# Attention and gated MLP: the opening of the kernel in finer steps

## The chip, the core and the metric

One core of a Trainium2 chip runs the whole program. The metric is the device time of one execution in microseconds (us); smaller is better. Engines are named as in the profile: PE is TensorE (PEld its weight loads), DVE is VectorE, ACT is ScalarE, POOL is GpSimd, SP is SyncE, which here only issues DMAs, in a fixed order, each at its turn.

## What is computed

Causal attention over 4 batches of 12 heads (448 positions, head size 64, fp32), followed by a gated MLP on the 1792 tokens of 768 features. The scales of `q` and `k` don't change the work.

```python
scores = scale * np.matmul(q, k.transpose(0, 1, 3, 2))
scores = np.where(mask, -1000000000.0, scores)          # causal
attn = np.exp(scores - max); attn = attn / (sum(attn) + 1e-09)
out = np.matmul(attn, v)
x = out.transpose(0, 2, 1, 3).reshape(4 * 448, 768)
gate = 1.0 / (1.0 + np.exp(-(x @ w_gate)))
result = (gate * (x @ w_val)) @ w_out
```

## The kernel before

**Units of work.** Attention goes by pairs of heads, 24 pairs, 6 to a batch. The MLP goes by batches: batches 0 and 1 each as a unit of its own (lines 582 to 653), 2 and 3 together (from line 720). Each product of the MLP is three matmuls, because x and the weights are split into a high and a low part (line 594).

**A pair, in the opening.** The six pairs of batch 0 are the opening; nothing of the MLP can run before their features are there. For a pair, `load` (L274, L279) fetches the queries and keys into `raw` and an extra piece into `sm`, `load_v` (L285) the values into `vr`. `products` (L387) computes four blocks of scores, i = 0 to 3, for 128 queries each (64 for the last) against 128, 256, 384 and 448 keys, for both heads z. Blocks 0 and 1 share one PSUM tile per head and are one step of PE; blocks 2 and 3 are steps of their own. `softmax` then has, per block and head, one masking and maximum on DVE (L410), one exponential on ACT (L417), and per pair two reciprocals of the sums on DVE (L426, L428) and a scaling on POOL (L438). `trans` (L313) transposes the scaled blocks in four groups g of four 128x128 squares into a PSUM tile `t`, of which there are two, and `empty` (L319 to L324) copies each group from PSUM to `pt` in SBUF, on ACT for the groups in the tuple `EV` (line 39) and on DVE for the others. `pv` (L337, L342) multiplies by the values, and `features` copies the result out as `xh` (ACT, L355) and the remainder `xl` (DVE, L356).

**Later pairs** (from pair 6) compute all four blocks in one step (`wscore`), and `shift` transposes on DVE (L453) and through DRAM: one write to `pd` (L461), four reads into `pt` (L464). `wpv` (L481) multiplies by the values.

**Weights.** `weight` (from line 548) fetches a 64-bit weight tile (L559), puts its two words together (ACT L563, DVE L565 and L567), stores the fp32 tile to `wdram` for the second unit (L570), and splits it (ACT L575, then POOL or DVE L577).

**The order.** Every operation is put into `Plan` with a cost, the buffers that it reads and writes with keys inside them, and a due time. `Plan.order` (line 156) pulls due times back from successors, adds the entries of `NUDGE` by the number of the operation, and then picks on each engine the ready operation that is due first. The instructions are issued to each engine in the order found; the waits come from the buffers. Since operations are numbered as they are put in, a table `NUDGE` holds for one list of operations alone.

```python
cols = (0, 4 * WQ, 2 * S) if n == 0 else (0, 2 * S)      # line 271: the first pair's load in two pieces
EV = (1, 3)                                              # line 39: groups of transposes that ACT copies
```

Of the kernel before, what the change touches and what calls it, by code (L numbers as in the profile page):

```python
# [15 lines left out]
B, H, S, D = 4, 12, 448, 64  # L16
# [21 lines left out]
WC = 512  # L38
EV = (1, 3)
BUFS = dict(w64=3, wd=2, wr=3, ws=3, sm=4, raw=3, pt=2, gt=5, vr=2, st=4, tb=1)  # L40
# [7 lines left out]
NUDGE = {  # L48
# [7 lines left out]
}  # L56
# [151 lines left out]
def kernel(  # L208
# [59 lines left out]
    def load(n):  # L268
        j = pairs[n]
        j["raw"] = r = new("raw", [128, 2 * S], F32, BUFS["raw"])  # L270
        cols = (0, 4 * WQ, 2 * S) if n == 0 else (0, 2 * S)
        for e, (a, c) in enumerate(zip(cols, cols[1:])):
            keys_ = (e,) if n == 0 else (0, 1)
            plan.op("SP", dma(128 * (c - a) * 4), lambda a=a, c=c: nc.sync.dma_start(  # L274
                out=r.t[:, a:c], in_=qkt[n][:, a:c]), writes=[(r, *keys_)], extra=2.8)
# [12 lines left out]
    def score(n, blocks, due):  # L288
# [8 lines left out]
        j["sp"].update({i: (sp, woff(i) - woff(blocks[0])) for i in blocks})  # L297
        needs = [(j["raw"], *((0,) if blocks[-1] == 1 else (0, 1)))] + ([(j["sm"][1], "x")] if blocks[-1] == 3 else [])
        burst((qk_cost(blocks), lambda: products(j, blocks), needs, [(p,) for p in sp]), due)
        return lambda: softmax(j, blocks)  # L300
# [69 lines left out]
    def products(j, blocks):  # L370
        r, x = j["raw"], j["sm"][1]
        first = r is pairs[0]["raw"]
        q0 = lambda i: WQ * i + (S if first and i > 1 else 0)
        k0 = 2 * WQ if first else S
        for i in blocks:
# [13 lines left out]
    def wscore(n, due):  # L389
# [4 lines left out]
        j["sp"] = {0: (a, 384), 1: (b, 0), 2: (a, 0), 3: (b, 256)}  # L394
        burst((1.95, lambda: products(j, range(NB)), [(j["raw"], 0, 1), (j["sm"][1], "x")], [(p,) for p in a + b]), due)
        return lambda: softmax(j, range(NB))

    def softmax(j, blocks):
        mn, su, r_ = j["mn"], j["sum"], j["r"]
        for i in blocks:  # L400
# [4 lines left out]
            for z in range(2):  # L405
# [6 lines left out]
                    op0=ALU.add, op1=ALU.min, accum_out=mn.t[:, to, i:i + 1],  # L412
                ), [(sp[z],), (mask, "end") if last and z else (mask,)] + ([(mn, (1, i))] if last and z else []),
                    [(sm, (i, z) if last else i), (mn, (to, i))])
            for z in heads:
                sm = j["sm"][z]
                plan.op("ACT", act(ne, 0, 1) + 0.01, lambda z=z, sm=sm, i=i, ne=ne, off=off: nc.scalar.activation(  # L417
                    out=sm.t[:, off:off + ne], in_=sm.t[:, off:off + ne], func=ACTF.Exp, scale=-1.0,
                    bias=mn.t[:, z, i:i + 1], accum_out=su.t[:, z, i:i + 1],
                ), [(mn, (z, i))], [*([(sm, (i, 0), (i, 1))] if last else []), (sm, i), (su, (z, i))], extra=0.1)  # L420
# [625 lines left out]
def _lay(q, k, v, moe_w_gate, moe_w_val, moe_w_out):  # L1046
# [5 lines left out]
    x = qkt[0].copy()  # L1052
    qkt[0] = np.concatenate([x[:, :2 * WQ], x[:, S:], x[:, 2 * WQ:S]], axis=1)
    qkt = np.concatenate([qkt, ex], axis=2)
# [40 lines left out]
```

## Time and profile before

| what | before |
| --- | --- |
| median of 3 runs | 622.55 us (621.22 to 623.70) |
| the profiled execution's own time | 620.8 us |
| its span in the profile | 619.1 us |
| granted clock of PE | 1.00 in every stretch |
| busy share of PE, PEld, DVE, ACT, POOL | 98%, 86%, 71%, 54%, 50% |

The profiled execution took 1.7 us more than its span, which is what lies around the first and the last instruction. A busy share is an average over the opening, the middle and the end of the program, which have different limits; the stretches have to be read one by one. Times in rows are us from the start of the span.

### The profile page before, as it was taken

What the parts mean: (1) busy time and instruction counts of PE and PEld (TensorE: products, weight loads), DVE (VectorE), ACT (ScalarE), POOL (GpSimd) and SP (SyncE); (2) the same over time, 40 slices, a digit from 0 to 9 for tenths busy, and PEclk for the clock granted to TensorE, in tenths of its full rate; (3) what the DMA queues carried; (4) which work ended last, traced back from release to release, by engine and by line L of the source; (5) the groups of instructions that cost most, each with busy time, mean ns of one, the idle gap of its engine ahead of it and who ended that gap; (6) DMA issues with size and microseconds to landing.
All of it is one profiled execution on the core that took longest, in us unless ns stands there. A gap on an engine that the chain in (4) does not pass through costs nothing.

```text
span 619.1 us, 11867 instructions
## 1 busy us (share of the span) xinstructions
PE 606.9 (98%) x4182; PEld 531.5 (86%) x4182; DVE 439.7 (71%) x1048; ACT 335.6 (54%) x754; POOL 310.6 (50%) x350
## 2 busy tenths in 40 slices
PE   6999999999999999999999999999999999999997
PEld 3578888898888888888888899989999989999996
DVE  5897999889855546544648766577754688999752
ACT  6996765675634755555558644434333443657420
POOL 5650534614300676767676676658664666611200
PEclk9999999999999999999999999999999999999999
DMA  8688999998999999878786886855533213534321
GB/s 299 203 308 314 344 370 378 376 397 320 364 396 339 321 365 344 293 245 319 269 323 247 281 311 238 276 199 189 179 110 95 77 52 103 159 117 142 112 75 60
DMA packets 54348, 153.35 MB, mean 248 GB/s; under 512 B 6032, under 2 KB 12432, under 8 KB 51984
## 3 DMA queue, kind: packets, MB, share of 16 engines
q1 hardware_dynamic: 54288, 152.59, 69.6%
q8 instruction: 33, 0.54, 0.3%
q14 instruction: 27, 0.22, 0.1%
HBM read 109.31 MB, written 43.25 MB: 246 GB/s over the span
## 4 chain that ended last, share of the span: by engine, by line
PE 89%; DMA 4%; DVE 3%; ACT 2%; issue 1%; POOL 0%; SPq 0%; DVEq 0%; ACTq 0%; POOLq 0%
PE m L594 39%; PE m L807 19%; PE s L807 10%; PE t L807 7%; PE m L481 5%; PE s L387 4%; PE t L387 2%; DMA raw<-in_qkt_dram 2%; DMA pd<-tb 1%; DMA vr<-in_vt_dram 1%; PE t L313 1%; ACT sm L417 1%; DVE wr L567 1%; DVE sm L410 1%; POOL sm L438 0%
## 5 line engine op out<-in xcount | busy, mean ns | idle before, releaser
L761 POOL TENSOR_TENSOR wl<-room,wh 128x384 fp32r<-128x384 f32 x84 | 98.0, 1190 | 56.0 <-ACT wh L760 56.0
L438 POOL TENSOR_SCALAR sm<-sm,r 128x384 f32<-128x384 f32 (+3 forms) x165 | 94.1, 591 | 63.6 <-DVE r L428 50.2
L594 PE MATMUL m<-xh,wh 128*128 128x448 f32 x288 | 107.3, 372 | 0.0
L594 PE MATMUL m<-xh,wl 128*128 128x448 f32 x288 | 105.3, 366 | 0.0
L594 PE MATMUL m<-xl,wh 128*128 128x448 f32 x288 | 105.2, 365 | 0.0
L417 ACT ACTIVATE sm<-sm,mn 128x384 f32<-128x384 f32 (+3 forms) x168 | 87.6, 524 | 18.6 <-DVE mn L410 15.2
L577 POOL TENSOR_TENSOR wl<-wr,wh 128x768 fp32r<-128x768 f32 x38 | 70.6, 1872 | 24.1 <-ACT wh L575 20.8
L575 ACT CAST wh<-wr 128x768 fp32r<-128x768 f32 x72 | 59.8, 832 | 33.4 <-DVE wr L567 15.0
L760 ACT CAST wh<-room 128x384 fp32r<-128x384 f32 x84 | 39.8, 511 | 52.5 <-PE s L807 12.7
L410 DVE CUSTOM_DVE_ANT_0 sm<-s,mask 128x128 f32<-128x128 f32 (+3 forms) x108 | 42.5, 408 | 25.8 <-PE s L387 25.7
L594 PEld LDWEIGHTS m<-xh,wh 128*128 128x128 f32 x288 | 54.1, 188 | 6.6 <-issue 1.6
L594 PEld LDWEIGHTS m<-xh,wl 128*128 128x128 f32 x288 | 54.1, 188 | 4.5
L594 PEld LDWEIGHTS m<-xl,wh 128*128 128x128 f32 x288 | 54.1, 188 | 4.1
L594 PE MATMUL m<-gh,wh 128*128 128x448 f32 x144 | 53.3, 370 | 0.0
L594 PE MATMUL m<-gh,wl 128*128 128x448 f32 x144 | 52.6, 365 | 0.0
L594 PE MATMUL m<-gl,wh 128*128 128x448 f32 x144 | 52.6, 365 | 0.0
L624 POOL TENSOR_TENSOR gl<-gt,gh 128x448 fp32r<-128x448 f32 x24 | 28.9, 1208 | 37.4 <-ACT gh L623 27.3
L807 PE MATMUL m<-pt,wh 128*128 128x448 f32 x150 | 44.8, 367 | 0.2 <-DVE xl L676 0.2
L453 DVE STREAM_TRANSPOSE room<-sm 128x384 f32<-128x384 f32 (+2 forms) x84 | 35.4, 449 | 8.8 <-POOL sm L438 8.4
L387 PE MATMUL s<-raw 64*64 64x128 f32 (+3 forms) x432 | 35.7, 390 | 4.6 <-DMA raw<-in_qkt_dram 3.5
L481 PEld LDWEIGHTS m<-pt,vr 128*64 128x64 f32 x720 | 33.5, 137 | 7.8 <-issue 4.3
L577 DVE TENSOR_TENSOR wl<-wr,wh 128x768 fp32r<-128x768 f32 x34 | 33.5, 984 | 7.9 <-ACT wh L575 7.4
(177 smaller groups left out, 1373.7 us busy)
## 6 DMA issues: line engine op xcount, KB each, us to landing
room<-in_wp_dram SPq DMA_DIRECT2D x36, 768.0 KB, 7.4
pt<-pd SPq DMA_DIRECT2D x72, 256.0 KB, 5.6
wr<-wdram SPq DMA_DIRECT2D x45, 384.0 KB, 4.6
room<-wdram SPq DMA_DIRECT2D x45, 384.0 KB, 3.6
wdram<-wr SPq DMA_DIRECT2D x36, 384.0 KB, 7.6
pd<-room SPq DMA_DIRECT2D x12, 1024.0 KB, 4.7
raw<-in_qkt_dram SPq DMA_DIRECT2D x23, 448.0 KB, 5.9
vr<-in_vt_dram SPq DMA_DIRECT2D x24, 256.0 KB, 5.3
```

What stands on the lines that cost most here:

```text
L387: nc.tensor.matmul(out=sp[z].t[c:c + 64, o:o + ne], lhsT=q, rhs=k)
L410: plan.op("DVE", dve(n), lambda z=z, i=i, sp=sp, sm=sm, n=n, o=o, f=f, lo=lo, to=to, first=first: nc.vector.tensor_tensor_reduce(out=sm.t[ ...
L417: plan.op("ACT", act(ne, 0, 1) + 0.01, lambda z=z, sm=sm, i=i, ne=ne, off=off: nc.scalar.activation(out=sm.t[:, off:off + ne], in_=sm.t[:, ...
L438: plan.op("PL", 0.24 + w / 1200, lambda sm=sm, e=e, o=o, w=w, z=z: nc.gpsimd.tensor_scalar(out=sm.t[:, o:o + w], in0=sm.t[:, o:o + w], sca ...
L453: plan.op("DVE", dve(128 * c) + 0.03, lambda sm=sm, i=i, o=o, c=c, at=at: nc.vector.transpose(out=tv()[:, :, at:at + 32 * c].rearrange("p ...
L481: nc.tensor.matmul(out=vp.t[64 * z:64 * z + 64, i * WQ:i * WQ + rows(i)], lhsT=v.t[:, c, z], rhs=src, start=(c == 0), stop=(c == i))
L575: plan.op("ACT", act(768), lambda: nc.scalar.copy(hi_.t, t.t), [(t,)], [(hi_,)])
L577: plan.op(eng, cost, lambda: at.tensor_tensor(out=lo_.t, in0=t.t, in1=hi_.t.bitcast(F32), op=ALU.subtract), [(t,), (hi_,)], [(lo_,)], lock ...
L594: nc.tensor.matmul(out=ps.t[:, :S], lhsT=a.t[:, k, :], rhs=b.t if isinstance(b, Buf) else b(), start=(first and z == 0), stop=(last and z ...
L760: plan.op("ACT", act(w), lambda: nc.scalar.copy(f(hi_.t), x()), [(src, at)], [(hi_, e)])
L761: plan.op("PL", 0.97, lambda: nc.gpsimd.tensor_tensor(out=f(lo_.t), in0=x(), in1=f(hi_.t).bitcast(F32), op=ALU.subtract), [(src, at), (hi_ ...
L807: nc.tensor.matmul(out=ps.t[:, :S], lhsT=a.t[:, kw, :], rhs=b.at, start=bool(first and z == 0), stop=bool(last and z == 2), skip_group_che ...
```

## The change

The first pair's `qkt` is laid out on the host as 128 queries, all 448 keys, and the other 320 queries, and fetched in three DMAs: 256 columns (128 queries and 128 keys), 448 columns, 192 columns. Block 0 of the first pair is a step of PE of its own, due 0.3 us before block 1, and the scores' tile is tracked by blocks. `EV` is (1,): of the four groups of a pair in the opening ACT copies one and DVE three. The planner's cost of an exponential rises by 0.08 us. `NUDGE` is another table, since the operations are numbered anew.

```diff
-EV = (1, 3)
+EV = (1,)
...
-        cols = (0, 4 * WQ, 2 * S) if n == 0 else (0, 2 * S)
+        cols = (0, 2 * WQ, S + 2 * WQ, 2 * S) if n == 0 else (0, 2 * S)
...
-            keys_ = (e,) if n == 0 else (0, 1)
+            keys_ = (e,) if n == 0 else (0, 1, 2)
...
-        needs = [(j["raw"], *((0,) if blocks[-1] == 1 else (0, 1)))] + ([(j["sm"][1], "x")] if blocks[-1] == 3 else [])
-        burst((qk_cost(blocks), lambda: products(j, blocks), needs, [(p,) for p in sp]), due)
+        needs = lambda i: [(j["raw"], *range(min(i + 1, 3)))] + ([(j["sm"][1], "x")] if i == 3 else [])
+        if n < 1 and len(blocks) > 1:
+            for i in blocks[:-1]:
+                plan.op("PE", qk_cost((i,)), lambda i=i: products(j, (i,)), needs(i), [(p, i) for p in sp], due - 0.3)
+        here = blocks[-1:] if n < 1 else blocks
+        burst((qk_cost(here), lambda: products(j, here), needs(here[-1]), [(p, *here) for p in sp]), due)
...
-                ), [(sp[z],), (mask, "end") if last and z else (mask,)] + ([(mn, (1, i))] if last and z else []),
+                ), [(sp[z], i), (mask, "end") if last and z else (mask,)] + ([(mn, (1, i))] if last and z else []),
...
-                plan.op("ACT", act(ne, 0, 1) + 0.01, lambda z=z, sm=sm, i=i, ne=ne, off=off: nc.scalar.activation(
+                plan.op("ACT", act(ne, 0, 1) + 0.09, lambda z=z, sm=sm, i=i, ne=ne, off=off: nc.scalar.activation(
...
-    qkt[0] = np.concatenate([x[:, :2 * WQ], x[:, S:], x[:, 2 * WQ:S]], axis=1)
+    qkt[0] = np.concatenate([x[:, :WQ], x[:, S:], x[:, WQ:S]], axis=1)
```

**What moves.** Lines of the change stand up to 3 lower or 1 higher than before (L387 is L390, L410 is L413, L274 is L273, L285 is L284). First place: PE at the start of the program, the scores of the first pair (`s` and `m` are PSUM tiles of scores, one per head, the number tells buffers apart; the brackets name the semaphores waited on). Before:

```order
L387 MATMUL s_315<-raw_289 64x128 [waits DMAHW0_49]
L387 MATMUL s_316<-raw_289 64x128
L387 MATMUL s_315<-raw_289 64x128
L387 MATMUL s_316<-raw_289 64x128
L387 MATMUL s_315<-raw_289 64x256
L387 MATMUL s_316<-raw_289 64x256
```

And of the change:

```order
L390 MATMUL s_316<-raw_289 64x128 [waits DMAHW0_49]
L390 MATMUL s_317<-raw_289 64x128
L390 MATMUL s_316<-raw_289 64x128
L390 MATMUL s_317<-raw_289 64x128
L390 MATMUL s_316<-raw_289 64x256 [waits DMAHW1_49,DVE_49]
L390 MATMUL s_317<-raw_289 64x256 [waits DVE_49]
```

The order is the same, but block 1 (256 keys) now waits for the second DMA and, since it writes to the tile that DVE reads block 0 from, for DVE.

Second place: SP's queue at the start, where every load stands. Before:

```order
L274 DMA raw<-in_qkt_dram 128x512
L274 DMA raw<-in_qkt_dram 128x384
L279 DMA sm<-in_qkt_dram 128x288
L274 DMA raw<-in_qkt_dram 128x896
L279 DMA sm<-in_qkt_dram 128x288
L285 DMA vr<-in_vt_dram 128x512
```

And of the change:

```order
L273 DMA raw<-in_qkt_dram 128x256
L273 DMA raw<-in_qkt_dram 128x448
L273 DMA raw<-in_qkt_dram 128x192
L278 DMA sm<-in_qkt_dram 128x288 x2
L284 DMA vr<-in_vt_dram 128x512 x2
L273 DMA raw<-in_qkt_dram 128x896 x3
```

The load of pair 1 (896 columns) was the fourth DMA and is the eighth, behind both extra pieces and both values.

Third place: SP's queue in the middle of unit 0, at the values of a later pair (the pair whose `pt` is read). Before:

```order
L461 DMA pd<-tb 128x2048
L559 DMA room<-in_wp_dram 128x1536 x2
L464 DMA pt<-pd 128x512 x4
L285 DMA vr<-in_vt_dram 128x512
L570 DMA wdram_2322<-wr 128x768
```

And of the change:

```order
L464 DMA pd<-tb 128x2048
L562 DMA room<-in_wp_dram 128x1536
L284 DMA vr<-in_vt_dram 128x512
L573 DMA wdram_2252<-wr 128x768
L562 DMA room<-in_wp_dram 128x1536
L467 DMA pt<-pd 128x512 x4
```

The values `vr` went ahead of the second weight and of the four reads of `pt`; at the pair after this one they did so too.

## Rows read from the trace of the kernel before

**Rows 1.** Busy time by stretch: stretch, length, engines with instructions, clock, DMA share, GB/s

```profile
core 0: us, PE busy (x) PEld busy (x) DVE busy (x) ACT busy (x) POOL busy (x), PEclk, DMA share, GB/s
0.00:15.00 15.00, 9.58 (x100) 5.74 (x100) 8.58 (x46) 10.27 (x32) 7.59 (x24) 1.00 0.86 300
...
5.20:47.62 42.42, 39.41 (x410) 25.99 (x404) 38.38 (x148) 38.70 (x112) 24.77 (x41) 1.00 0.83 284
...
54.20:180.00 125.80, 124.01 (x876) 109.81 (x874) 110.26 (x263) 81.60 (x169) 46.11 (x59) 1.00 0.97 362
180.00:360.00 180.00, 180.00 (x1487) 156.31 (x1487) 108.73 (x383) 103.52 (x264) 114.63 (x140) 1.00 0.87 309
```

**Rows 2.** Timeline, 0 to 30 us: start, length, engine, line, operation, [idle before <-releaser]

```profile
0.80 0.86 SPq L274 DMA_DIRECT2D raw<-in_qkt_dram  x2
...
2.18 0.43 SPq L274 DMA_DIRECT2D raw<-in_qkt_dram  x1
...
3.47 1.56 PE L387 MATMUL s<-raw 64*64 64x128 f32 x16 [3.47 <-DMA raw<-in_qkt_dram]
...
5.20 0.29 DVE L410 CUSTOM_DVE_ANT_0 sm<-s,mask 128x128 f32<-128x128 f32 x1 [5.20 <-PE s L387]
...
5.62 0.42 DVE L410 CUSTOM_DVE_ANT_0 sm<-s,mask 128x256 f32<-128x256 f32 x1
...
6.36 0.56 DVE L410 CUSTOM_DVE_ANT_0 sm<-m,mask 128x384 f32<-128x384 f32 x1
...
8.93 0.25 DVE L410 CUSTOM_DVE_ANT_0 sm<-s,mask 128x128 f32<-128x128 f32 x1
```

**Rows 3.** DMA issues of the first pairs: KB each, us from issue to landing

```profile
raw<-in_qkt_dram SPq DMA_DIRECT2D x1, 256.0 KB, 2.6
...
raw<-in_qkt_dram SPq DMA_DIRECT2D x1, 192.0 KB, 2.6
...
raw<-in_qkt_dram SPq DMA_DIRECT2D x1, 448.0 KB, 5.1
```

**Rows 4.** Timeline, one copy on DVE and one on ACT, each with its follower

```profile
32.37 0.69 DVE L324 COPY pt<-t 128x512 f32<-128x512 f32 x1
...
32.62 0.57 ACT L322 COPY pt<-t 128x512 f32<-128x512 f32 x1
...
33.02 0.39 DVE L410 CUSTOM_DVE_ANT_0 sm<-s,mask 128x224 f32<-128x224 f32 x1
33.09 0.62 ACT L417 ACTIVATE sm<-sm,mn 128x384 f32<-128x384 f32 x1
```

**Rows 5.** Timeline, the end of the opening: last copies, and the last two products with values

```profile
46.93 0.69 DVE L324 COPY pt<-t 128x512 f32<-128x512 f32 x1
...
47.26 1.52 PE L337 MATMUL s<-pt,vr 128*64 128x384 f32 x12
47.37 0.59 ACT L322 COPY pt<-t 128x512 f32<-128x512 f32 x1 [0.48 <-PE t L313]
...
49.07 1.47 PE L337 MATMUL s<-pt,vr 128*64 128x384 f32 x12
```

**Rows 6.** Timeline of PE, the two longest waits behind the opening

```profile
162.59 2.00 PE L481 MATMUL m<-pt,vr 128*64 128x128 f32 x40 [1.23 <-DMA vr<-in_vt_dram]
...
179.94 2.00 PE L481 MATMUL m<-pt,vr 128*64 128x128 f32 x40 [0.56 <-DMA vr<-in_vt_dram]
```

**Rows 7.** SP's queue in the timeline (values' issues), and the chain (last `pt` issue)

```profile
155.64 0.47 SPq L285 DMA_DIRECT2D vr<-in_vt_dram  x1
...
171.99 1.38 SPq L464
...
173.41 0.44 SPq L285 DMA_DIRECT2D vr<-in_vt_dram  x1
```

**Rows 8.** DMA issues at 155.2, 155.6, 172 and 173.4 us: KB each, us to landing

```profile
pt<-pd SPq DMA_DIRECT2D x1, 256.0 KB, 6.8
...
vr<-in_vt_dram SPq DMA_DIRECT2D x1, 256.0 KB, 6.9
...
pt<-pd SPq DMA_DIRECT2D x1, 256.0 KB, 7.2
...
vr<-in_vt_dram SPq DMA_DIRECT2D x1, 256.0 KB, 6.4
```

More of the change, by code (lines that the diff above doesn't have):

```diff
@@ L372, in products @@
         first = r is pairs[0]["raw"]
-        q0 = lambda i: WQ * i + (S if first and i > 1 else 0)
-        k0 = 2 * WQ if first else S
+        q0 = lambda i: WQ * i + (S if first and i else 0)
+        k0 = WQ if first else S
         for i in blocks:
@@ L394, in wscore @@
         j["sp"] = {0: (a, 384), 1: (b, 0), 2: (a, 0), 3: (b, 256)}
-        burst((1.95, lambda: products(j, range(NB)), [(j["raw"], 0, 1), (j["sm"][1], "x")], [(p,) for p in a + b]), due)
+        burst((1.95, lambda: products(j, range(NB)), [(j["raw"], 0, 1, 2), (j["sm"][1], "x")], [(p, 0, 2) for p in a] + [(p, 1, 3) for p in b]), due)
         return lambda: softmax(j, range(NB))
```

13 rows, old and new, of the table NUDGE are left out of this document.

## Prediction

> **What bounds the kernel now.** I read the busy time by stretch first, then the waits of PE, then the timeline of the opening, then the DMAs at the two places where PE waits. The stretches show three stages [rows 1]. From 180 us on PE is busy for the whole of 180.00 us out of 180.00: nothing to win there, only to lose. From 54 to 180 us PE is idle for 125.80 - 124.01 = 1.8 us, and the DMA engines are busy for 0.97 of the time at 362 GB/s: this stage is close to the limit of the DMAs, and 1.23 + 0.56 = 1.8 us of PE's idle time stands before two products that wait for the values of their pair [rows 6]. The opening, from DVE's first softmax operation at 5.20 us to the end of DVE's last copy at 47.62, is 42.42 us long; in it PE is idle for 3.0 us, DVE for 4.0 and ACT for 3.7 [rows 1]. So three engines there are over 90% busy and wait for each other in turn; none has room for much more, and PE could win 3.0 us at the very most. The granted clock is 1.00 throughout, the upper of its two levels (2.4 GHz), so the clock explains nothing here.
>
> Two lengths cannot be moved much, therefore: the opening, and the two waits of 1.8 us. All that the change can win is 3.0 + 1.8 us and what the first load saves, about 5 us or 0.8%.
>
> **First load.** Before, 256 KB land 2.6 us after their issue and 192 KB also 2.6 us [rows 3]. The first piece is now 128 KB. From the two equal rows the gain is 0; from the rate of the first stretch, 300 GB/s [rows 1], 128 KB less are 0.44 us. I take 0.2, between the two. [...]
>
> **Block 0 alone.** PE starts at 3.47 and DVE's first operation at 5.20 [rows 2]. The order of waits shows why: DVE had to wait for seven matmuls, four of block 0 and three of block 1. These took 1.73 us. Four of seven by count would be 0.99 us, by columns (512 of 1280) 0.69; I take 0.8 and DVE starts at 3.47 - 0.2 + 0.8 = 4.1, which is 1.1 us sooner. But PE now waits for DVE: block 1 writes to the tile that DVE still reads. DVE needs 0.21 us per head (two rows of block 0 between 5.20 and 5.62) [rows 2], so block 1 starts at about 4.3, needs the other 0.9 us, and DVE goes on at 5.2 to 5.3 instead of 5.62. Block 2 now comes behind that on PE. Its three matmuls of 384 columns have 1152 columns against 1280 in 1.73 us, so 1.0 to 1.5 us, and DVE gets to block 2 at 6.3 to 6.8; before it was 6.36 [rows 2]. So what is won at the first operation is spent at the third: by then DVE has waited about 1.1 us that it did not wait before. Net for the first pair 0, between -0.3 and +0.4.
>
> **Pair 1's load goes back in the queue.** It was issued at 2.18 and landed at 2.18 + 5.1 = 7.3 us [rows 2, 3], with 592 KB issued ahead of it. Now 1248 KB are ahead. At 300 GB/s [rows 1] the 656 KB more cost 2.2 us, so it lands at up to 9.5; if the DMAs issued behind it shared the time before as well, the least is about 8.5. DVE began pair 1 at 8.93, when the scores were long there [rows 2]. PE needs about 0.9 us for the two blocks, so DVE begins pair 1 at 9.5 to 10.4 instead. I take a wait of 0.9 us for DVE and ACT.
>
> **Six copies from ACT to DVE.** A copy ends its turn on DVE after 33.02 - 32.37 = 0.65 us and on ACT after 33.09 - 32.62 = 0.47 us [rows 4]. Six pairs, one copy each: DVE gets 3.9 us more, ACT 2.8 us less. ACT's relief only helps if ACT was what the others waited for. Here a rule speaks against the change. The Trainium skill (Perfetto Trace Analysis, Optimizing Scalar/DVE Operations) gives DVE a larger overhead per access to PSUM than ScalarE (about 125 against 51 ns) and advises to offload from DVE to Scalar when DVE is saturated; the rows agree with its order, and by it this edit would be a loss, which is the second rival below.
>
> **The sum for the opening.** DVE's work from its first operation to its last copy was 38.4 us [rows 1]; it is now 38.4 + 3.9 = 42.3. The weights' operations on DVE and ACT inside the opening only move to later places in it; their number up to the last copy is the same. From 4.1 us on, without any idle time, the last copy would end at 46.4. I add the 1.1 us of the first pair, the 0.9 us of the second and 0.4 us for the other four, because a queue that always has a copy ready hardly runs dry (in the last 12 us of the opening DVE already works like this). That is 48.8. Before, the last copy, on ACT, ended at 47.37 + 0.59 = 47.96, and the last product with values began at 49.07, held up by the one before it on PE [rows 5]. It now begins at 48.8: the opening wins **0.3 us**. With the 4.0 us of idle time that DVE has now [rows 1] added to the two new waits it would end at 46.4 + 1.1 + 0.9 + 3.7 = 52.1 and lose 3.0; with PE's idle time all gone it would win 3.0 + 0.2. Those are the ends.
>
> **The values ahead of `pt`.** Two products waited for `vr`, which was issued behind the four reads of `pt` [rows 6, 7]. The first `vr` went out at 155.64 and landed 6.9 us later, at 162.5; the last `pt` went out at about 155.2 and landed 6.8 us later, at 162.0 [rows 7, 8]. Without the wait for `vr` the next to be late is `pt`, so 0.5 of the 1.23 us goes. At the second place `vr` landed at 173.41 + 6.4 = 179.8 and the last `pt` at 171.99 + 7.2 = 179.2 [rows 7, 8]; all of the 0.56 us goes. Sum **1.1 us**, at most 1.8 if `pt` also comes sooner, and 0 if in the full DMA stage another transfer becomes late in their place. In the change the values also stand ahead of a weight that held up the queue.
>
> All else in the new due times I cost at nothing: behind 180 us PE has work at hand always, and a place more or less in its order costs nothing as long as the weights come in time; if they don't, the price is a new wait like those two, 0.5 to 1.2 us each.
>
> Together -0.3 - 1.1 = -1.4 us against the profiled execution's 620.8, so 619.4. The median of the three runs is 622.55, 1.75 us above that execution; on its scale the forecast is **621.1 us**.
>
> **The rivals.** (All on the median's scale.)
>
> - *PE bound in the opening* (0.27). DVE takes the copies without holding anyone up, ACT's 2.8 us are what the others had waited for, and PE loses its 3.0 us of idle time. For it: PE's work in the opening is 39.4 of 42.4 us, and DVE's order now mixes copies with softmax more finely. Against it: DVE's sum above. Time: -3.0 - 0.2 - 1.1 to -1.8, about 618.0.
> - *DVE too full* (0.20). Every copy that PE waits for (there are two `t` tiles, so the third group of a pair waits for the copy of the first) stands behind softmax on one engine. It decides from the point at which DVE's last copy ends later than 49.1 us. With today's idle time kept the last copy ends at 52.1 and the time is +3.0, 625.6; with the gain at `vr` 624.5, with pair 1's load later still 626.5.
> - *Given back* (0.15). The opening ends sooner, but the stage to 180 us runs at the pace of the DMAs (0.97 busy) and PE waits at the same places until the same data are there. Then the time is that of before, 622.5. Against it: the weights' loads are tied to the opening's progress and come sooner with it.
>
> **How the numbers follow.** My forecast has 0.38, with a range of its own from 619.9 to 622.3. 0.5% is 3.1 us, about what a measurement of this kernel can tell from no change. Faster by more than that needs 619.4 or less: the first rival, 0.27. Slower by more needs 625.7: of the second rival somewhat over half, 0.13. The rest, 0.60, is within 0.5%. The range for 8 times in 10 takes in most of the first rival and the nearer part of the second: 617.4 to 625.0.
>
> **What would show it.** In the profile after: DVE's first operation near 4.1 us and a wait of DVE for PE right behind it; pair 1's load landing at 8.5 to 9.5 and DVE's first operation of pair 1 behind 9.5; DVE's idle time in the opening down to 2.4 us from 4.0; the last copy at about 48.8 and the last product with values right behind; no wait for `vr` near 160 and 179 us, and a short one for `pt` in its place. I am wrong on DVE if its idle time stays near 4 us or the last copy ends before 47; wrong on the full DMA stage if PE's idle time from the end of the opening to 180 us is again 1.8 us or more; and wrong on all that I cost at nothing if PE is no longer busy all the time behind 180 us.

## The result: 0.56% slower, and the profile after

Over 8 executions each, the median went from 621.95 to 625.33 us; the ratio is 1.0056, with a 95% interval of 1.0034 to 1.0078. That is 3.4 us more, where 1.4 us less had been forecast. The profiled execution of the change took 625.79 us with a span of 624.1 (before 619.1). In the tables "6th product" is the start on PE of the sixth pair's product with values, which ends the opening (before 49.07 [rows 5]).

Busy time by stretch in the change (stretch, length, engines with instructions, granted clock, DMA share, GB/s); the last two lines, from a narrower query, show the clock behind PE's longest wait:

```profile
0.00:15.00 15.00, 9.11 (x76) 5.31 (x76) 6.97 (x35) 7.82 (x24) 5.80 (x19) 0.89 0.81 268
15.00:55.00 40.00, 38.61 (x437) 26.49 (x436) 37.37 (x122) 31.14 (x86) 22.36 (x34) 1.00 0.76 250
54.20:180.00 125.80, 124.64 (x886) 109.50 (x879) 110.53 (x263) 79.67 (x167) 41.97 (x59) 1.00 0.96 362
340.00:390.00 50.00, 47.73 (x347) 42.66 (x346) 39.34 (x89) 26.50 (x63) 29.37 (x28) 1.00 0.74 265
...
10.00:11.00 1.00, 1.00 (x20) 0.66 (x23) 0.25 (x2) 0.00 (x0) 1.00 (x3) 0.85 1.02 292
11.00:12.00 1.00, 1.00 (x9) 0.10 (x2) 0.79 (x6) 0.87 (x4) 1.00 (x3) 0.50 0.90 304
```

Three places differ from [rows 1]. From 0 to 15 us the granted clock is 0.89 instead of 1.00, and in 11 to 12 us it is 0.50, the lower level (1.2 GHz). From 54.2 to 180 us PE's idle time fell from 1.8 to 1.16 us. And from 340 to 390 us PE, which before was busy there without a gap (first row below), is idle for 2.27 us (50.00 - 47.73). Three rows of the kernel before, to set beside those of the change:

```profile
340.00:390.00 50.00, 50.00 (x360) 45.08 (x359) 35.36 (x73) 26.42 (x59) 33.62 (x30) 1.00 0.76 269
...
7.31 0.88 PE L387 MATMUL m<-raw 64*64 64x384 f32 x8 [0.46 <-DMA raw<-in_qkt_dram]
...
330.89 0.68 DVE L686 TENSOR_TENSOR tb<-xl,tb 128x448 fp32r<-128x448 f32 x1 [0.24 <-ACT tb L681]
```

The timeline of the change, PE's and DVE's rows of the opening and the new waits:

```profile
2.99 0.71 PE L390 MATMUL s<-raw 64*64 64x128 f32 x8 [2.99 <-DMA raw<-in_qkt_dram]
4.22 1.33 PE L390 MATMUL s<-raw 64*64 64x256 f32 x8 [0.53 <-DVE mn L413]
9.88 0.88 PE L390 MATMUL s<-raw 64*64 64x128 f32 x16 [2.38 <-DVE r L429]
10.55 1.43 PE L390 MATMUL m<-raw 64*64 64x384 f32 x8
51.36 1.47 PE L340 MATMUL s<-pt,vr 128*64 128x384 f32 x12
...
3.87 0.29 DVE L413 CUSTOM_DVE_ANT_0 sm<-s,mask 128x128 f32<-128x128 f32 x1 [3.87 <-PE s L390]
5.60 0.42 DVE L413 CUSTOM_DVE_ANT_0 sm<-s,mask 128x256 f32<-128x256 f32 x1 [1.22 <-PE s L390]
6.88 0.56 DVE L413 CUSTOM_DVE_ANT_0 sm<-m,mask 128x384 f32<-128x384 f32 x1 [0.50 <-PE m L390]
10.80 0.29 DVE L413 CUSTOM_DVE_ANT_0 sm<-s,mask 128x128 f32<-128x128 f32 x1 [0.75 <-PE s L390]
...
367.04 0.47 PE L597 MATMUL m<-gh,wl 128*128 128x448 f32 x1 [1.04 <-POOL wl L580]
379.06 2.00 PE L484 MATMUL m<-pt,vr 128*64 128x128 f32 x40 [1.22 <-DMA out_dram<-gt]
...
510.28 0.47 PE L810 MATMUL t<-xh,wh 128*128 128x448 f32 x1 [0.63 <-ACT xh L837]
```

The opening starts sooner: PE at 2.99 (before 3.47), DVE at 3.87 (before 5.20 [rows 2]). It has lost that at block 1 (5.60, before 5.62) and more at block 2 (6.88, before 6.36). Pair 1 begins on PE at 9.88 instead of 7.31 and on DVE at 10.80 instead of 8.93. The name behind the arrow of the 2.38 us wait can't be right (that operation of DVE belongs to pair 0); what PE waits for there is pair 1's load, as the rows of other runs say. The sixth product is 2.3 us late, and two new waits, of 1.04 and 1.22 us, stand before 367 and 379 us. Again the second releaser is only the last that came: the wait is for `pt`, which that product reads. A third one, of 0.63 us, stands at 510 us; in the whole of 390 to 619 us PE before had one of 0.2 us.

### The profile page after: what moved, and what is told of

It is laid out like the page before. It is cut to its first block, busy times and chain, and to the rows that moved or that the text cites. A ratio compares the mean times of both kernels' runs of the same rounds, so it can differ in the third digit from the quotient of the medians.

```text
span 624.1 us, 11872 instructions
## 1 busy us (share of the span) xinstructions
PE 609.1 (98%) x4182; PEld 532.5 (85%) x4182; DVE 447.0 (72%) x1054; ACT 332.0 (53%) x748; POOL 304.2 (49%) x350
## 4 chain that ended last, share of the span: by engine, by line
PE 82%; DVE 8%; POOL 3%; DMA 2%; issue 2%; ACT 2%; SPq 0%; DVEq 0%; POOLq 0%; ACTq 0%
PE m L597 31%; PE m L810 19%; PE s L810 11%; PE t L810 7%; PE m L484 4%; PE s L390 4%; POOL sm L441 2%; DVE wr L570 2%; PE t L390 2%; DVE sm L413 2%; PE t L316 2%; DMA room<-in_wp_dram 1%; DVE wr L568 1%; POOL wl L580 1%; DMA out_dram<-gt 1%
## 5 line engine op out<-in xcount | busy, mean ns | idle before, releaser
L764 POOL TENSOR_TENSOR wl<-room,wh 128x384 fp32r<-128x384 f32 x84 | 96.5, 1168 | 60.5 <-ACT wh L763 57.2
L441 POOL TENSOR_SCALAR sm<-sm,r 128x128 f32<-128x128 f32 (+3 forms) x165 | 89.2, 561 | 68.1 <-DVE r L431 46.6
L420 ACT ACTIVATE sm<-sm,mn 128x128 f32<-128x128 f32 (+3 forms) x168 | 87.6, 524 | 20.1 <-DVE mn L413 19.7
L413 DVE CUSTOM_DVE_ANT_0 sm<-s,mask 128x128 f32<-128x128 f32 (+3 forms) x108 | 42.5, 408 | 21.0 <-PE s L390 21.0
L390 PE MATMUL s<-raw 64*64 64x128 f32 (+3 forms) x432 | 37.5, 394 | 6.2 <-DMA raw<-in_qkt_dram 3.0
```

Of the source, the lines that this page charges most:

```text
L390: nc.tensor.matmul(out=sp[z].t[c:c + 64, o:o + ne], lhsT=q, rhs=k)
L413: plan.op("DVE", dve(n), lambda z=z, i=i, sp=sp, sm=sm, n=n, o=o, f=f, lo=lo, to=to, first=first: nc.vector.tensor_tensor_reduce(out=sm.t[ ...
L420: plan.op("ACT", act(ne, 0, 1) + 0.09, lambda z=z, sm=sm, i=i, ne=ne, off=off: nc.scalar.activation(out=sm.t[:, off:off + ne], in_=sm.t[:, ...
L441: plan.op("PL", 0.24 + w / 1200, lambda sm=sm, e=e, o=o, w=w, z=z: nc.gpsimd.tensor_scalar(out=sm.t[:, o:o + w], in0=sm.t[:, o:o + w], sca ...
L764: plan.op("PL", 0.97, lambda: nc.gpsimd.tensor_tensor(out=f(lo_.t), in0=x(), in1=f(hi_.t).bitcast(F32), op=ALU.subtract), [(src, at), (hi_ ...
```

## The experiments

The planner's order changes everywhere when one cost or entry changes. So these kernels have their order written out: a list of the operations' numbers, as the planner had found it for the kernel before or for the change, in place of `order = plan.order()`. Edits to a list are shown as rows of the one queue that changes. Ratios are to the kernel before on the same chip.

| run | ratio (95% interval) | 6th product, us | PE idle 340 to 390, us |
| --- | --- | --- | --- |
| the kernel before | 1 | 49.07 | 0 |
| the change | 1.0056 (1.0034 to 1.0078) | 51.36 | 2.27 |
| a_then_b | 1.0022 (0.9995 to 1.0048) | 49.19 | 0 |
| b_then_a | 1.0035 (1.0018 to 1.0053) | 49.30 | 2.25 |
| a_raw1 | 1.0031 (1.0013 to 1.0049) | 49.12 | 2.27 |
| b_late1 | 1.0025 (1.0007 to 1.0043) | 51.72 | 0 |
| a_warm | 1.0148 (1.0103 to 1.0194) | 57.69 | 1.18 |
| a_warm2 | 1.0021 (1.0001 to 1.0041) | 49.86 | 0 |
| a_ev13 | 1.0063 (1.0041 to 1.0084) | 51.49 | 2.44 |
| b_vr | 0.9979 (0.9963 to 0.9996) | 49.20 | 0 |
| b_mid | 0.9991 (0.9980 to 1.0001) | 49.13 | 0 |
| b_vr_split | 0.9998 (0.9983 to 1.0013) | 49.62 | 0 |
| a_pool | 1.0040 (1.0017 to 1.0063) | 51.04 | 0 |
| a_fix | 1.0004 (0.9985 to 1.0023) | 49.14 | 0 |
| b_dve | 1.0027 (1.0003 to 1.0050) | 49.20 | 1.34 |
| b_pool | 1.0004 (0.9988 to 1.0019) | 49.26 | 0.62 |
| b_both | 1.0044 (1.0028 to 1.0061) | 49.16 | 0.88 |
| a_dve | 1.0030 (1.0017 to 1.0043) | 51.30 (a_dve2) | 0 (a_dve2) |

### Opening or order behind it: a_then_b and b_then_a

Both orders hold the same operations up to the sixth product, but for two, so they can be joined there.

```diff
-    order = plan.order()
+    order = CHANGE[:upto(sixth_product)] + [o for o in BEFORE if o not in that part]
```

(b_then_a is the other way round, on the code of the kernel before.) Expected of a_then_b:

> The change (its load, its scores, its copies) in its own order up to the sixth product with values, and in the order of the kernel before from there. Theory 'opening alone': the whole loss stays, sixth product at 51.4, ratio 1.005 to 1.006, PE without idle time from 180 to 385 us. Rival 'order behind': about 2.3 us of loss stays, ratio 1.003 to 1.004. Third case: the DMA-bound stage up to 180 us takes the delay in (the weights' loads go on while the opening is late), ratio 1.000 to 1.002 with the two waits for vr shorter than 1.8 us together.

Expected of b_then_a:

> The kernel before (its load, its scores, its copies) in its own order up to the sixth product with values, and in the order of the change from there. Theory 'opening alone' (all of the loss is made in the opening, and the new order behind it wins the 1.1 us of the waits for vr): sixth product at 49.1, ratio 0.998 to 0.999. Rival 'order behind' (new waits behind 180 us for a weight's low part and for pt cost 1.0 and 1.2 us, besides about 0.6 us in smaller ones): ratio 1.0015 to 1.0035, PE idle for about 2 us between 340 and 385 us.

The two ratios, 0.22% and 0.35%, add up to the change's 0.56%, with intervals of about 0.2% to either side. "Opening alone" has fallen: with the opening of before, the new order alone loses 0.35%, with the same 2.25 us of idle time from 340 to 390 us. a_then_b came out between its cases, with an interval that reaches 1. In its one trace pair 1's data came sooner, and the sixth product lost next to nothing.

```profile
9.18 0.88 PE L390 MATMUL s<-raw 64*64 64x128 f32 x16 [1.67 <-DVE r L431]
9.86 0.85 PE L390 MATMUL m<-raw 64*64 64x384 f32 x8
```

PE waited 1.67 us instead of 2.38, the eight rows of 384 columns took 0.85 us instead of 1.43, and the sixth product began 2.2 us sooner than in the change. Data that were 0.7 us sooner are not worth 2.2 us by themselves; the rate of the matmuls behind the wait has to be in it.

That execution took 623.19 us all the same, and lost its time elsewhere: near 164 us PE waited for 2.19 us, and from 166 to 168 us the granted clock was 0.50. The kernel before seems to do so too, now and then. Of 132 of its executions beside these runs 25 have a mean granted clock of 0.995 to 0.997, and their median is 624.2 us; the others have 0.999 or 1.000, and 621.2 us. Four traces of orders with `vr` behind `pt` show the place (a_then_b, b_late1, b_dve, b_both): a wait of 1.95 to 3.11 us at the product that waited for 1.23 us in [rows 6], and the lower clock behind it. Of b_both:

```profile
163.40 2.98 PE L481 MATMUL m<-pt,vr 128*64 128x128 f32 x40 [1.95 <-DMA vr<-in_vt_dram]
...
164.00:166.00 2.00, 2.00 (x32) 2.00 (x30) 1.64 (x3) 0.00 (x0) 0.00 (x0) 0.54 0.98 385
166.00:168.00 2.00, 2.00 (x12) 1.74 (x10) 1.25 (x3) 1.57 (x3) 0.00 (x0) 0.60 1.07 441
```

In b_then_a, b_vr and b_mid, which have the opening of before and `vr` ahead of `pt`, none of 35 executions has such a mean. "At the full clock" means below: the executions with 0.999 or more alone. Of a_then_b's these are 7 of 12, and their median is 0.5 us above that of the kernel before (29 executions), so its 0.22% cannot all be put down to the opening.

### Pair 1's load: a_raw1 and b_late1

a_raw1 moves that one DMA in the order of the change; b_late1 does the reverse in the order before, where the second values have to go ahead too.

```diff
 L278 sm<-in_qkt_dram (pair 0)
+L273 raw<-in_qkt_dram (pair 1)
 L278 sm<-in_qkt_dram (pair 1)
 L284 vr<-in_vt_dram (pairs 0 and 1)
-L273 raw<-in_qkt_dram (pair 1)
```

> The change in its own order, with one DMA moved: pair 1's load of queries and keys is issued fifth, behind the first pair's extra piece, and not eighth. Theory 'load' (pair 1's data are late, PE has nothing to do for 2.4 us and its granted clock falls right after): PE begins pair 1 at 7.3 to 8.2 us instead of 9.88, the granted clock of 9.8 to 15 us is 1.00 again, the product with values of the sixth pair begins at 49.1 to 49.9 instead of 51.36, and the ratio to the kernel before is 1.002 to 1.003 instead of 1.0056. Rival 'copies' (DVE is full from 24 us on and sets the end of the opening whatever happens at 8 us): the sixth product still begins at 50.8 or later and the ratio stays at 1.005.

For b_late1:

> The kernel before with two DMAs moved: pair 1's load of queries and keys is issued behind both extra pieces and both values, as in the change; its own load, scores and copies stay. Theory 'load': PE waits about 2 us for pair 1 (begins at 9.0 to 9.9 instead of 7.31), the matmuls behind that wait may run at half the rate, the sixth product with values begins at 50.0 to 51.4 instead of 49.07, ratio 1.002 to 1.005. Rival (the loss of the opening comes from block 0 alone or from the copies, and pair 1's lateness is taken up by the idle time that PE has until 50 us): sixth product within 0.6 us of 49.07, ratio 0.999 to 1.001.

In a_raw1 PE began pair 1 at 8.03, the clock stayed at 1.00, the sixth product began at 49.12, and the ratio fell by 0.25%, as theory "load" said. The intervals of the two ratios overlap, so it is the rows that decide. Of a_raw1:

```profile
8.03 1.63 PE L390 MATMUL s<-raw 64*64 64x128 f32 x16 [0.46 <-DVE mn L413]
...
49.12 1.47 PE L340 MATMUL s<-pt,vr 128*64 128x384 f32 x12
```

b_late1 shows the loss in an order with nothing else of the change. Its PE row and its stretches:

```profile
9.41 1.14 PE L387 MATMUL m<-raw 64*64 64x384 f32 x8 [2.44 <-DMA raw<-in_qkt_dram]
```

```profile
9.80:12.00 2.20, 2.20 (x26) 1.28 (x18) 0.14 (x1) 0.00 (x0) 2.20 (x6) 0.52 1.02 417
12.00:15.00 3.00, 2.79 (x28) 1.35 (x26) 3.00 (x18) 2.81 (x11) 0.70 (x2) 0.78 0.89 322
```

A wait of 2.44 us, then a granted clock of 0.52, and the sixth product at 51.72, 2.65 us late; over all executions +0.25%.

### Is it the rate? a_warm and a_warm2

Both put matmuls that nobody reads ahead of pair 1's scores, into the tile that these overwrite. a_warm:

```diff
+        if j is pairs[1] and blocks[0] == 0:
+            x0 = pairs[0]["raw"].t
+            for _ in range(6):
+                nc.tensor.matmul(out=j["sp"][0][0][0].t[:64, :S], lhsT=x0[:64, :64], rhs=x0[:64, WQ:WQ + S])
```

> The change with six more matmuls of 64x448 on PE ahead of pair 1's scores, on the first pair's data and into the tile that pair 1's scores then overwrite; nothing reads them. They run in the 2.4 us in which PE waits for pair 1's load. Theory 'rate' (PE's wait is followed by a stretch of matmuls at half the rate, 1.43 us instead of 0.88 for the eight of 384 columns, and that costs 1 to 2 us beside the wait itself): with PE busy in the wait the eight matmuls take 0.85 to 0.95 us, the granted clock stays at 1.00 up to 15 us and the sixth product begins at 49.3 to 50.4 instead of 51.36; ratio 1.0035 to 1.005. Rival (only the lateness of the data counts): the sixth product at 51 or later, ratio 1.005 to 1.006.

This was mis-sized: the six took 9 us, and pair 1 waited for them. It still showed something (PE's rows):

```profile
7.07 8.42 PE L381 MATMUL s<-raw 64*64 64x448 f32 x11
...
16.95 1.85 PE L394 MATMUL m<-raw 64*64 64x384 f32 x8
```

PE was busy from 4 to 17 us, yet eight rows of 384 columns still took 1.85 us. a_warm2 has three matmuls of the whole array instead:

```diff
-            for _ in range(6):
-                nc.tensor.matmul(out=j["sp"][0][0][0].t[:64, :S], lhsT=x0[:64, :64], rhs=x0[:64, WQ:WQ + S])
+            for _ in range(3):
+                nc.tensor.matmul(out=j["sp"][0][0][0].t[:, :HALF], lhsT=x0[:, :WQ], rhs=x0[:, WQ:WQ + HALF])
```

> The change with three matmuls of 128x128 by 224 columns on PE ahead of pair 1's scores, on the first pair's data, into a tile that pair 1's scores then overwrite; nothing reads them. At half the rate they take 2.2 us, which fits into PE's wait for pair 1 (7.5 to 9.88 us); the six matmuls of the earlier run used one 64x64 corner and took 0.76 us for half of one, 9 us in all, so that run held pair 1 up by itself. Theory 'rate': with PE at work in the wait pair 1 begins at 9.8 to 10.1, its eight rows of 384 columns take 0.85 to 0.95 us instead of 1.43, granted clock 1.00 to 15 us, sixth product at 49.3 to 50.2, ratio 1.0035 to 1.005. Rival (the lower rate behind 9.9 us has another cause, or the data alone count): 1.2 us or more for the eight, sixth product at 51 or later.

```profile
7.50 1.40 PE L381 MATMUL s<-raw 128*128 128x224 f32 x6
9.90 0.88 PE L394 MATMUL s<-raw 64*64 64x128 f32 x16 [1.00 <-DMA raw<-in_qkt_dram]
10.60 0.83 PE L394 MATMUL m<-raw 64*64 64x384 f32 x8
```

Pair 1's data came as late as in the change (9.90 against 9.88), and the sixth product began at 49.86 instead of 51.36. So, by these three traces, 1.5 us of the 2.24 us that the late load costs there (51.36 - 49.12) go with the lower rate, and 0.74 us with the wait itself; a_raw1's first sixteen rows were at the lower rate too (1.63 us), though its clock reads 1.00. This run also had no wait behind 340 us, so its ratio is not the opening's alone.

### The copies: a_ev13

```diff
-EV = (1,)
+EV = (1, 3)
```

> The change in its own order, with the fourth copy of each pair of the opening issued to ACT again (EV = (1, 3)), at the same place of the order. Theory 'load': the copies cost little, pair 1 still begins at 9.9 on PE with the lower clock behind it, the sixth product begins within 0.7 us of 51.36, ratio 1.0045 to 1.006. Rival 'copies': DVE has 3.9 us less to do from 13 us on, the sixth product begins at 49 to 50, ratio 1.002 to 1.003.

Theory "load" holds, rival "copies" has fallen. In the 40 us from 15 us on DVE had 2.5 us less to do and ACT 3.0 more than in the change, PE the same, and nothing moved at the end of the opening.

```profile
15.00:55.00 40.00, 38.59 (x438) 26.07 (x436) 34.86 (x120) 34.18 (x92) 22.45 (x34) 1.00 0.77 250
```

With the load early it is the same: the sixth product at 49.14 with the copies on ACT (a_fix, below) and at 49.12 with them on DVE (a_raw1).

### The values ahead of `pt`: b_vr and b_mid

b_vr is the kernel before with the two loads of values moved; b_mid takes the order of the change from the sixth product to the product near 185 us only.

```diff
 L461 pd<-tb
 L559 room<-in_wp_dram
+L285 vr<-in_vt_dram
 L559 room<-in_wp_dram
 L464 pt<-pd x4
-L285 vr<-in_vt_dram
```

> The kernel before with two DMAs moved: at the two places near 155 and 172 us the load of the values vr is issued ahead of the four reads of pt. It is the prediction's second term alone. The prediction's step: no wait for vr there, a short one for pt, 1.1 us less (0 to 1.8), ratio 0.998. Rival (pt waits for the same transfers, now with 256 KB ahead of it in a stage where the DMAs are busy for 0.97 of the time): pt is late by as much as vr was, PE's idle time from 55 to 180 us stays at 1.5 us or more, ratio 0.999 to 1.002.

For b_mid:

> The kernel before in its own order up to the sixth product with values, in the order of the change from there to the product near 185 us, and in its own order again behind that. Theory 'order behind 180 costs, order to 180 wins': PE's idle time from 55 to 180 us is 1.1 to 1.2 us instead of 1.8, none from 185 to 385 us, ratio 0.998 to 0.9995. Rival (the loss of 0.35% that the order of the change made behind the opening comes from the middle stage): ratio 1.002 or more.

b_vr won 0.21%, 1.3 us (0.2 to 2.3); the prediction's term was 1.1. It is the one version that is clearly faster than the kernel before. Of its waits between 54.2 and 180 us none is for `vr` or at the second place:

```profile
PE m L481 <- issue: 0.7, 1, 0.7
PE m L594 <- DVE wl L577: 0.6, 1, 0.6
```

The two waits of 1.79 us have become one of 0.7, as forecast, but the 0.6 us for a weight are new, so PE's idle time in this stage fell by 0.5 us only (1.79 to 1.32). At the full clock b_vr won 0.7 us (12 executions against 24); the rest of its 1.3 us is that none of its executions had the lower mean clock, which 5 of 29 of the kernel before had.

b_mid won 0.6 us (its interval just reaches 1): the change's order brings three small waits for weights into the same stage (0.5, 0.3 and 0.3 us) and one of 0.5 us for `pt`. They take back half or more.

### Three pieces and block 0 alone: b_vr_split

b_vr with the first load and the scores of the change, and with block 1's step behind DVE's reads of block 0, as there:

```diff
-        cols = (0, 4 * WQ, 2 * S) if n == 0 else (0, 2 * S)
+        cols = (0, 2 * WQ, S + 2 * WQ, 2 * S) if n == 0 else (0, 2 * S)
...
+        if n < 1 and len(blocks) > 1:
+            for i in blocks[:-1]:
+                plan.op("PE", qk_cost((i,)), lambda i=i: products(j, (i,)), needs(i), [(p, i) for p in sp], due - 0.3)
```

> The kernel before with the values ahead of pt at two places (alone: ratio 0.9979), and besides the first load in three pieces and block 0 as a step of its own, as in the change; pair 1's load stays fifth, copies and all else as before. Prediction's step (what is won at the first operation is spent at the third; net -0.3 to +0.4 us): DVE's first operation at 3.9 us, its block 2 at 6.8 to 6.9, sixth product at 48.8 to 49.5, ratio 0.9973 to 0.9985. Rival (the earlier start carries through to the end of the opening): sixth product at 48.5 or earlier, ratio 0.9965 or less.

The sixth product began at 49.62, against 49.20 in b_vr: the sooner start is gone by the third block, and 0.4 us more. The total (0.9998) doesn't tell itself from 1 nor, by the intervals, from b_vr; what this part is worth over all executions stays open.

### The waits behind 340 us: a_pool, a_fix, and a 2 by 2 table

In the order of the change a weight's low part stands ahead of a pair's seven scalings on POOL. a_pool moves it back, and on SP the write of `pd` ahead of two DMAs:

```diff
-L580 wl<-wr,wh
 L441 sm<-sm,r x7
+L580 wl<-wr,wh
```

> The change in its own order, with three operations moved near 340 to 365 us: the low part of one weight goes behind a pair's seven scalings on POOL again, as in the kernel before, and on SP the write of that group's transposed scores goes ahead of a weight's read and an output's write that it stood behind. Theory 'one weight in front of the scalings' (it waits on POOL for a cast that ACT makes behind the pair's last exponential, and holds the scalings, the transposes, DVE's next softmax and the next pair's pt up by 4 us): the two waits of PE near 371 and 378 us (1.0 and 1.2 us) go, PE's idle time from 340 to 390 us falls from 2.27 us to under 0.5, and the ratio is 1.002 to 1.004 instead of 1.0056. Rival (other moves of the new order make these waits): the idle time stays at 1.5 us or more, ratio 1.005 to 1.006.

The waits went, as theory "one weight" wanted. But the trace had another difference that the move doesn't explain, 7 us ahead of it: a subtraction on DVE took 2.00 us where the change has 4.88. And from 180 to 340 us PE was idle for 1.27 us (0.97 in a_fix), where both kernels have nothing. a_fix joins a_pool, a_raw1 and a_ev13:

> The change in its own order, with three parts undone together: pair 1's load issued fifth, the fourth copy of each pair on ACT again, and the three operations near 350 us as in the run before this. Theory 'additive' (load 0.25%, order behind 180 us 0.35%, copies nothing): ratio 0.9985 to 1.0005, sixth product within 0.3 us of the 49.12 that it had with the early load alone. Rival 'copies, once the load is early' (with the load early DVE is the bound of the opening, and 3.9 us less on it count): sixth product at 48.5 or earlier, ratio 0.996 to 0.998.

It came out at 1.0004, where the sum of the parts puts it, although the subtraction kept its late place. To tell the two causes apart, each was put into the kernel before alone (b_dve, b_pool) and both together (b_both), and the subtraction was moved back in the change (a_dve). The move on DVE:

```diff
 L453 room<-sm x2
-L686 tb<-xl,tb
 L453 and L456 room<-sm x6
+L686 tb<-xl,tb
```

> The kernel before with one operation moved: near 331 us the subtraction tb<-xl,tb on DVE (line 686) goes behind the eight transposes of a pair, where the change has it, from behind the first two. Theory 'DVE and POOL' (there it starts while POOL has three subtractions of two SBUF tiles ready one behind the other, and does not finish until POOL is through; the pair's softmax then starts 2 to 3 us late): it takes 2.0 to 4.9 us instead of 0.68, the pair's POOL scalings start 1 to 3 us later than 341.4, PE idle from 340 to 390 us 0.3 to 2.2 us, ratio 1.000 to 1.0035. Rival 'POOL move alone': the subtraction takes under 1 us or its delay is taken in, no idle time of PE from 340 to 390 us, ratio 0.999 to 1.001.

For b_pool:

> The kernel before with three operations moved as the change has them: near 341 us one weight's low part goes ahead of a pair's seven scalings on POOL, and the write of a pair's transposed scores on SP goes behind a weight's read and an output's write. Theory 'POOL move alone': the scalings start at 344 to 346 us instead of 341.4, PE is idle for 1.5 to 2.3 us from 340 to 390 us, ratio 1.0025 to 1.0035. Rival 'DVE and POOL': the cast that the weight waits for is done early enough, PE idle under 0.5 us there, ratio 0.999 to 1.001.

For b_both:

> The kernel before with both moves, the one on DVE near 331 us and the three near 341 us. Theory 'both are needed': this run alone of the three shows what the order of the change shows: the subtraction at 4.88 us, PE idle for about 2.2 us from 340 to 390 us, ratio 1.002 to 1.0035. If one move alone does it, this run is no worse than that one. If neither does, PE's idle time there stays under 0.5 us and other moves of the order are the cause.

For a_dve, and for a_dve2, the same kernel, whose rows are shown in its place:

> The change in its own order with one operation moved back: the subtraction tb<-xl,tb on DVE behind the pair's first two transposes, as before. The opening is left as it is (pair 1's load late). Theory 'DVE and POOL': it takes 0.6 to 0.8 us, the pair's softmax starts 2 us earlier and PE's idle time from 340 to 390 us falls from 2.27 to under 0.5 us; ratio 1.002 to 1.004. Rival 'POOL move alone': idle time there 1.5 us or more, ratio 1.005 to 1.006.

> The change with the one subtraction on DVE moved back behind the first two transposes, a second time, for its trace. Theory 'DVE and POOL': the subtraction takes 0.6 to 0.8 us near 333 us, PE's idle time from 340 to 390 us is under 0.7 us instead of 2.27. Rival: the subtraction is short and PE still waits for 1.5 us or more there.

Both moves take part, and the subtraction's costs more. It alone costs the kernel before 0.27% (b_dve), the moves on POOL and SP alone nothing that can be told from 1 (b_pool; PE idle 0.62 us), both 0.44%; and taken out of the change the subtraction's move leaves 1.0030 and no wait. But these ratios also hold the longer wait near 164 us, which stands ahead of anything that was moved: 5 of 11 executions of b_dve have the lower mean clock that goes with it, 2 of 12 of b_pool and 7 of 12 of b_both, against 10 of 34 of the kernel before. At the full clock the medians lie 1.3, 0.9 and 1.8 us above that of the kernel before (6, 10 and 5 executions against 24). And undoing the moves on POOL and SP, with the subtraction left late, took 0.16% off the change (a_pool) and, with the load early, 0.27% (from a_raw1 to a_fix, which also has the copies on ACT), each with an uncertainty of about 0.3%. How the loss divides between the two is therefore not shown. The rows, first of the change (DVE's, then POOL's), then of a_dve2, b_dve and a_pool:

```profile
335.08 4.88 DVE L689 TENSOR_TENSOR tb<-xl,tb 128x448 fp32r<-128x448 f32 x1
...
331.45 3.36 POOL L441 TENSOR_SCALAR sm<-sm,r 128x384 f32<-128x384 f32 x7 [5.62 <-DVE r L431]
334.78 1.83 POOL L580 TENSOR_TENSOR wl<-wr,wh 128x768 fp32r<-128x768 f32 x1
336.56 1.15 POOL L627 TENSOR_TENSOR gl<-gt,gh 128x448 fp32r<-128x448 f32 x1
337.65 1.83 POOL L580 TENSOR_TENSOR wl<-wr,wh 128x768 fp32r<-128x768 f32 x1
...
361.16 4.05 POOL L441 TENSOR_SCALAR sm<-sm,r 128x384 f32<-128x384 f32 x7 [5.87 <-DVE r L431]
```

```profile
333.73 0.69 DVE L689 TENSOR_TENSOR tb<-xl,tb 128x448 fp32r<-128x448 f32 x1 [0.24 <-ACT tb L684]
...
331.74 3.73 POOL L441 TENSOR_SCALAR sm<-sm,r 128x384 f32<-128x384 f32 x7 [5.64 <-DVE r L431]
```

```profile
338.73 4.59 DVE L686 TENSOR_TENSOR tb<-xl,tb 128x448 fp32r<-128x448 f32 x1
```

```profile
336.04 2.00 DVE L689 TENSOR_TENSOR tb<-xl,tb 128x448 fp32r<-128x448 f32 x1
...
335.74 1.83 POOL L580 TENSOR_TENSOR wl<-wr,wh 128x768 fp32r<-128x768 f32 x1
337.51 1.53 POOL L627 TENSOR_TENSOR gl<-gt,gh 128x448 fp32r<-128x448 f32 x1
```

Behind the eight transposes of the change the subtraction starts 0.3 us after POOL has begun three subtractions of its own, and ends at 339.96, half a microsecond after the last of them (337.65 + 1.83 = 339.48). Ahead of six of the transposes it meets POOL's seven scalings, and takes 0.69 us, while they take 3.73 us instead of 3.36. The Trainium skill (SBUF — State Buffer, Who interferes with whom) says that a DVE instruction with two SBUF inputs contends with a GpSimd instruction that reads SBUF, over a pair of ports that is locked for one of them, and that the order of issue decides which one blocks. The rows agree that the two hold each other up, but the order goes further: the subtraction, which was there before POOL's second and third instruction, was passed over by all three. From there the delay runs on in one chain: the pair's softmax on DVE, its scalings on POOL (5.87 us of idle time in front of the next pair's, 3.86 before), the weights behind them, `wr`'s buffers, SP's queue, `pt`. Whether the late place costs so much differs by execution: in the ten traces that have it the subtraction took 4.6 to 4.9 us seven times and 2.00 us three times (a_warm2, a_pool, a_fix), when only one instruction passed it over, and these three are the ones without the waits. In a_pool as in the change it starts 0.30 us behind POOL's first subtraction, so what decides between the two lengths is not shown.

## Why the prediction was wrong

- **"All else in the new due times I cost at nothing."** This is the step that failed most. b_then_a less b_mid, 0.44%, is 2.7 us. Two moved places, a subtraction's on DVE and a weight's on POOL, cost the kernel before 0.44% too, but 1.8 us at the full clock (b_both), so what else is in the 2.7 us stays open; the new wait at 510 us is about 0.4 us of it. The prediction had named what would prove it wrong, PE no longer busy all the time behind 180 us, and had the price of a wait right (0.5 to 1.2 us each; they were 1.04 and 1.22). It reasoned that PE has work at hand always and considered only late DMAs; that DVE and POOL can hold each other up, and that a pair's whole chain then comes late, it left out, though the planner's own flag `lock` marks these operations.
- **"Pair 1's load goes back in the queue."** Right in kind, too small in size. The forecast was that it lands at 8.5 to 9.5 and costs 0.9 us; PE began pair 1 between 9.18 and 9.90 in the runs with that queue, and undoing it gave back 0.25%, 1.6 us (2.2 us at the sixth product in the traces). What was missed is the rate: the granted clock of 1.00 throughout was taken to explain nothing, but it was read from an execution in which PE had no such wait (0.46 us at 7.31).
- **"Six copies from ACT to DVE" and the sum for the opening.** The sum went along DVE's queue (46.4 + 1.1 + 0.9 + 0.4 = 48.8). DVE did get busier, but the end did not depend on it: PE is busy for 38.6 of the 40 us from 15 us on with the copies on either engine. By the prediction's own sign it was wrong on DVE, whose idle time up to its last copy was to fall to 2.4 us: it is 5.7 (41.75 us of work in 47.49). That 48.8 lies near the 49.12 of a_raw1 is chance. The advice of the Trainium skill that spoke against the edit (Perfetto Trace Analysis, Optimizing Scalar/DVE Operations: off DVE when it is saturated) has the same order of prices as the rows of a copy (0.65 us on DVE, 0.47 on ACT) and decides nothing here. By the same token "DVE too full", whose 625.6 us is close to the result, is not what happened (and its 52.1 takes ACT's 3.7 us of idle time for DVE's 4.0, which would give 52.4), and "PE bound" named the right engine but found nothing to win, since PE's idle time from 15 to 55 us stayed at 1.4 us (before 1.1).
- **"First load", "block 0 alone".** 128 KB landed 2.1 us after their issue, 0.5 sooner than 256 KB [rows 3], not 0.2. "What is won at the first operation is spent at the third" held: block 1 at 5.60 (forecast 5.2 to 5.3), block 2 at 6.88 (6.3 to 6.8), 0.4 us late at the sixth product, the bad end of -0.3 to +0.4.
- **"The values ahead of `pt`."** Right in its mechanism: of the waits 0.7 us is left, as forecast. That the 1.3 us measured alone lies so near the 1.1 is in part luck, as 0.6 us came back at a weight and the longer waits of other executions, which the prediction's one trace didn't show, went too. In the change half or more of it went to other late weights, which the range (down to 0) had allowed.

Forecast -0.3 - 1.1 + 0; measured in the order of these parts +1.4 (a_then_b), -0.6 (b_mid) and +2.7, which is +3.5 against the 3.4 of the medians; each part is known to 0.6 us at best, so that it fits so well is chance. The time lies 0.3 us above the range: its upper end, 625.0, took in part of a loss in the opening, but nothing for late weights or a late `pt` behind 180 us.

## What to carry to other kernels

A list of new due times is not free because the bound engine has work at hand: go through the engines that share a resource (here DVE's two-input operations beside POOL's) and through the one queue of loads, and price each moved operation where it now meets another. A wait of a matmul engine is priced with the slower matmuls that may follow it, not by its length alone, and from several executions: one and the same wait was 1.23 us in one and 3.11 us in another here. Before moving work between two engines, check that the queue you add up is the one whose end the stage waits for.

## What the runs showed of the hardware

- The rate of matmuls can fall behind a wait, and the granted clock does not always show it. Behind waits of 2.38 us (the change) and 2.44 us (b_late1) the clock read 0.50 to 0.52. In a_ev13, behind 2.25 us, it read 1.00 from 9.8 to 15 us, while the first sixteen rows of pair 1 took 1.56 us instead of 0.88 and the eight of 384 columns 1.53 instead of 0.85 (second fence). The length of equal rows is the safer sign. The start of the program is such a case in every kernel here: the first eight rows of 384 columns take 1.50 us before and 1.71 in the change, at a clock that reads 1.00.
- The length of the wait alone does not decide it. Behind 2.29 us for `vr` (b_pool, first fence) the product took 2.00 us, as behind 1.23 us in [rows 6]; behind 1.95 us (b_both) it took 2.98 us.

```profile
164.27 2.00 PE L481 MATMUL m<-pt,vr 128*64 128x128 f32 x40 [2.29 <-DMA vr<-in_vt_dram]
```

```profile
9.82 1.56 PE L390 MATMUL s<-raw 64*64 64x128 f32 x16 [2.25 <-DMA raw<-in_qkt_dram]
11.13 1.53 PE L390 MATMUL m<-raw 64*64 64x384 f32 x8
...
9.80:15.00 5.20, 5.18 (x44) 3.08 (x44) 3.09 (x16) 2.39 (x9) 2.97 (x6) 1.00 0.92 342
```

- What PE does in the wait matters: three matmuls on the whole array were followed by the full rate (0.83 us), six on one 64x64 corner, busy for 9 us, were not (1.85 us).
- One subtraction on DVE took 0.69 us where it met POOL's scalings, and 2.00 or 4.88 us where it met POOL's subtractions, with the same 0.30 us between the two starts.
